# Batch 0's recurrent state summed by TensorE and decayed by ScalarE, pair 2's narrowing moved, late low-rank additions

## The chip, the cores and the metric

One core of one Trainium2 chip. The metric is the device time of one execution in microseconds; the kernel before has a median of 706.71 us over 3 runs (705.61 to 708.09).

## The reference, cut to what matters

The program is a gated linear attention over 4 batches, 8 heads, 768 positions and head dimension 48, followed by two mixing layers:

```python
f = 1 / (1 + exp(-f_logit))
for t in range(S):
    state = f[t][:, None] * state + outer(k[t], v[t])     # per batch and head, 48x48
    y[t] = q[t] @ state
x = heads side by side                                     # (B, 768, 384)
u = x + (x.transpose(0, 2, 1) @ U @ V).transpose(0, 2, 1)  # rank 32 over the positions
x = u + maximum(u @ w_ch1, 0) @ w_ch2                      # 384 -> 1536 -> 384
h = gelu(x @ w_in); u, v = halves of h                     # 384 -> 1024
x = x + (u * (w_sg @ layernorm(v) * g + b_sg)) @ w_out
```

Inputs are float32; the weights come as 64-bit words that hold doubles and are narrowed to float32 on the chip.

## The kernel before, in words

**Attention.** Each batch is cut into 6 chunks of 128 positions (NCH). Within a chunk the recurrence is turned into matrix products: two scans on VectorE, `a_decay` (L333, products of the forget gates backwards, g) and `a_grow` (L350, their inverse), scale k and q; `a_scores` multiplies k and q on TensorE (L365), masks the scores (`am`, VectorE L371, for batch 0 one half by ScalarE L373 and GpSimd L374) and transposes k (L379, L381). `a_out` forms y = am x v (L392) + q x T (L397), copies it to `x` (ScalarE, L400) and forms k'v (L412). T is the state, a tile of 112 partitions by 4 pairs of heads by 96 columns: head j of a pair stands in rows 64j to 64j+47 and columns 48j to 48j+47, all else in T is zero from the start (L186). `a_state` adds k'v to T (VectorE L426, one operation per j) and multiplies by the decay of the next chunk, `fall` (L428, one per j); in chunk 0 it only multiplies. `a_xt` transposes x into xT, and `low_rank_sum` adds x^T U into one PSUM bank (L458), whose sum after the last chunk becomes `hs`, high part on ScalarE (L468) and low part on VectorE (L469). `low_rank_out` then adds hs V to one half of the positions of xT in three products of 384 columns (L478) with an addition on VectorE each (L480). f32 products are run as two passes of the array, f32r products as one.

**Order.** The order of all instructions is written out by hand (`tc.manual_schedule`), each engine runs its own in order. For batch 0 the loop of L537 to L562 issues, for chunk c: the scans of chunk c+2, the scores of c+1, the transposition of c-1, the low-rank sum of c-2, the outputs and k'v of c, the state of c, and in between the narrowing of early weights: `use_first` (ScalarE L250 spreads the high words, VectorE L246 shifts the low ones), `use_middle` (VectorE L255, L256 merge them, two halves of 128x384 per pair), `use_last` (high part on ScalarE L285, low part on GpSimd L287). "Pair i" is the i-th of 12 pairs of w_ch1 and w_ch2 blocks of 128 hidden units. Pairs 1 and 2 are narrowed ahead of chunk 5's output. `warm(n)` issues n products with the identity that nobody reads (L520).

**MLP.** After the attention of batch 0 come the first low-rank additions, `make_hl` (the input's high parts on ScalarE L145 and low parts on VectorE L146), and the MLP of batch 0: per half of the positions 12 groups f; group f has 9 products into bank "h" (L80), a relu to `ah` (ScalarE L511), the low part `al` (VectorE L512), and the 9 products of the group before into three "ch" banks (L495). After each group `fill` issues more work. For batch 0 that is `narrow_ahead(f)`: the merge of pair f+3 out of PSUM, the high and low parts of pair f+2, the spread of pair f+4 into two "at" banks (L250) and its shift; from group 9 on also the attention of batch 1, which uses the old form of `a_state`. PSUM has 2 banks "h", 3 "ch" and 3 "at", each set used in turn.

Of the kernel before, what the change touches and what calls it, by code (L numbers as in the profile page):

```python
# [12 lines left out]
ACTF = mybir.ActivationFunctionType  # L13
# [4 lines left out]
B, H, S, D = 4, 8, 768, 48  # L18
# [3 lines left out]
NP = H // 2  # L22
# [4 lines left out]
KD = DM // 128  # L27
# [3 lines left out]
PR = 112  # L31
# [20 lines left out]
def kernel(  # L52
# [16 lines left out]
    vec, act, pool, pe = nc.vector, nc.scalar, nc.gpsimd, nc.tensor  # L69

    keep = ctx.enter_context(tc.tile_pool(name="keep", bufs=1))
    ident = keep.tile([128, 128], F32, name="ident")
# [59 lines left out]
    def fast(st):  # L132
# [7 lines left out]
        def bank(kind, shape):  # L140
            n = {"h": 2, "ch": 3, "at": 3}[kind]
            return ps.tile(shape, F32, tag=kind, bufs=n, name="ps_" + kind)

        def split(hi, lo, src, eng=pool):
            act.activation(hi, src, ACTF.Copy)  # L145
            eng.tensor_tensor(lo, src, hi.bitcast(F32), op=ALU.subtract)  # L146
# [6 lines left out]
        def make_hl(work, b, hf, eng=pool):  # L153
            hi = work.tile([128, KD, HT], F32R, tag="uh", name="uh")
            lo = work.tile([128, KD, HT], F32R, tag="ul", name="ul")
            for kd in range(KD):
                split(hi[:, kd], lo[:, kd], xT[b][:, kd, hf * HT:(hf + 1) * HT], eng)
            hl[b, hf] = (hi, lo)
# [23 lines left out]
        T = cst.tile([PR, NP, 2 * D], F32, name="T")  # L182
# [9 lines left out]
        def kind(b):  # L192
            return "at" if b else "ch"

        def room(b, c):
            if b == 0 and c > 2:
                x = flat(xT[6 - c])
                t, vv = x[0:PR, 0:QW], x[:, QW:QW + DM]
            else:
                t = ld.tile([PR, QW], F32, tag="fqk", name="fqk")  # L200
                vv = ld.tile([128, DM], F32, tag="v", name="v")
            tiles[b, c] = dict(t=t, v=vv)
            return t, vv

        def load(b, c):
            t, vv = room(b, c)
            for x in range(0, QW, QW // 2):
                nc.sync.dma_start(t[:, x:x + QW // 2], fqk[b, c, :, x:x + QW // 2])
            nc.sync.dma_start(vv, v[b, c * C:(c + 1) * C, :])
# [34 lines left out]
        def shift(i):  # L244
            for low, _ in raws[i]:
                vec.tensor_scalar(low, low, 29, None, op0=ALU.logical_shift_right)  # L246

        def spread(i, zs):
            for z, (_, high) in zip(zs, raws[i]):
                act.activation(z, high.bitcast(F32), ACTF.Copy, scale=2.0 ** -112)  # L250

        def merge(i, dst, zs):
            for d, z, (low, high) in zip(dst, zs, raws[i]):
                di, zi = d.bitcast(I32), z.bitcast(I32)
                vec.scalar_tensor_tensor(zi, zi, 3, low, op0=ALU.logical_shift_left, op1=ALU.bitwise_or)  # L255
                vec.scalar_tensor_tensor(di, high, -2 ** 31, zi, op0=ALU.bitwise_and, op1=ALU.bitwise_or)  # L256
# [3 lines left out]
        def z_tiles(i):  # L260
            z = zs.tile([128, 2, UNIT], F32, tag="z", name="z")
            n = NCH * R if i == "u" else UNIT
            return [z[:, x, :n] for x in range(len(raws[i]))]

        def use_first(i):
            ready[i] = z_tiles(i)
            spread(i, ready[i])
            shift(i)

        def use_middle(i):  # L270
            merge(i, ready[i], ready[i])
# [83 lines left out]
        def a_scan(b, c):  # L355
            a_decay(b, c)
            a_grow(b, c)
# [27 lines left out]
        def a_out(b, c):  # L385
            e = tiles[b, c]
            vv = e["v"]
            y = bank(kind(b), [128, DM])
            half = [slice(i, i + C // 2) for i in range(0, C, C // 2)]
            for h in range(H):  # L390
                for t in half:
                    pe.matmul(y[t, h * D:(h + 1) * D], lhsT=e["am"][h % 2][:, h // 2, t],  # L392
                              rhs=vv[:, h * D:(h + 1) * D], start=(h == 0), stop=(c == 0 and h == H - 1))
            if c:
                for p in range(NP):
                    for t in half:
                        pe.matmul(y[t, p * 2 * D:(p + 1) * 2 * D], lhsT=e["q"][:, p, t], rhs=T[:, p, :],  # L397
                                  start=False, stop=(p == NP - 1))
            x = aw.tile([128, DM], F32, tag="x", name="x", bufs=3)
            act.activation(x, y, ACTF.Copy)  # L400
            if b:
                xh[b, c] = aw.tile([128, DM], F32R, tag="xh", name="xh", bufs=3)
                xl[b, c] = aw.tile([128, DM], F32R, tag="xl", name="xl", bufs=3)
                split(xh[b, c], xl[b, c], x)
            else:
                xh[b, c] = x
            if c < NCH - 1:
                kv = bank(kind(b), [PR, NP, D])
                for p in range(NP):
                    for j in range(2):  # L410
                        rows = slice(64 * j, 64 * j + D)
                        pe.matmul(kv[rows, p, :], lhsT=e["kt"][:, p, rows],  # L412
                                  rhs=vv[:, (2 * p + j) * D:(2 * p + j + 1) * D], start=True, stop=True)
                e["kv"] = kv
            e["x"] = x

        def a_state(b, c):
            e = tiles[b, c]
            fall = tiles[b, c + 1]["fall"]
            parts = []  # L420
            for j in range(2):
                rows = slice(64 * j, 64 * j + D)
                parts.append((T[rows, :, j * D:(j + 1) * D], e["kv"][rows], fall[rows].to_broadcast([D, NP, D])))
            if c:
                for Tj, kv, _ in parts:
                    vec.tensor_tensor(Tj, kv, Tj, op=ALU.add)  # L426
            for Tj, kv, fj in parts:
                vec.tensor_tensor(Tj, Tj if c else kv, fj, op=ALU.mult)  # L428

        def a_xt(b, c):  # L430
            x = tiles[b, c]["x"]
            xp = bank(kind(b), [128, KD, C])
            for d in range(KD):
                pe.transpose(xp[:, d, :], x[:, d * 128:(d + 1) * 128], ident)
            act.activation(xT[b][:, :, c * C:(c + 1) * C], xp, ACTF.Copy)
            del tiles[b, c]
# [35 lines left out]
        def low_rank_out(b, hf, where="at"):  # L472
            for d in range(KD):
                low_rank_add(b, hf, d, where)

        def low_rank_add(b, hf, d, where):
            t = bank(where, [128, HT])
            pe.matmul(t, lhsT=hs[b][:, d * 128:(d + 1) * 128], rhs=vs[:, hf * HT:(hf + 1) * HT], start=True, stop=True)  # L478
            dst = xT[b][:, d, hf * HT:(hf + 1) * HT]
            vec.tensor_tensor(dst, t, dst, op=ALU.add)  # L480
# [36 lines left out]
        def warm(n, w=3):  # L517
            t = bank("h", [128, w, 128])
            for _ in range(n):
                pe.matmul(t, lhsT=ident, rhs=ident[:, None, :].to_broadcast([128, w, 128]), start=True, stop=True)  # L520
# [16 lines left out]
        for c in range(NCH):  # L537
            if c + 2 < NCH:
                a_scan(0, c + 2)
            if c - 1 in early:  # L540
                use_last(early[c - 1])
            if c + 1 < NCH:
                a_scores(0, c + 1)
            if c:
                a_xt(0, c - 1)
            if c > 1:
                low_rank_sum(0, c - 2)
            if c > 1 and c in early:
                use_first(early[c])
                use_middle(early[c])  # L550
            elif c == NCH - 1:
                low_rank_sum(0, c - 1)
                for i in (1, 2):
                    use_first(i)
                    use_middle(i)
            a_out(0, c)
            warm(1, 2)
            if c + 1 < NCH:
                a_state(0, c)
            if c == 0:  # L560
                use_first("u")
                use_middle("u")  # L562
        low_rank_sum(0, NCH - 1)
        use_last(1)
        a_xt(0, NCH - 1)
        warm(2)
        low_rank_out(0, 0)
        make_hl(work, 0, 0, vec)
        load(1, 0)
        load(1, 1)  # L570
        get(*range(3, KF1))
# [10 lines left out]
                load(nb, nc3)  # L582

        def narrow_ahead(f):
            if f == 0:
                low_rank_out(0, 1, "ch")
            if f + 3 < KF1:
                bank_middle(f + 3)
            if f + 2 < KF1:
                use_last(f + 2)  # L590
            if f + 4 < KF1:
                bank_first(f + 4)
# [371 lines left out]
```

## Time and profile before

| | |
|---|---|
| median of 3 runs | 706.71 us (705.61 to 708.09) |
| the profiled execution | 708.97 us, span 707.2 us, mean granted TensorE clock 0.986 |
| TensorE busy | 684.7 us (97%) |
| VectorE busy | 444.2 us (63%) |
| ScalarE, GpSimd busy | 260.1 us (37%), 242.3 us (34%) |
| attention of batch 0 | 0 to about 57 us |
| MLP of batch 0 begins | about 58.7 us |

The busy shares are means over the whole span; the stages differ. In the rows below PE is TensorE, PEld its weight loads, DVE VectorE, ACT ScalarE, POOL GpSimd. A row of the timeline merges instructions of one kind that follow each other (x2, x16), and the text in brackets is how long the engine idled before it and what released it. The clock is a share of the full 2.4 GHz.

### The profile page before, as it was taken

The numbers are of one execution on the slowest core, as the hardware profiler recorded it, in microseconds if no ns is written. First come the engines' busy times: TensorE is split into PE (matmuls) and PEld (weight loads), VectorE is DVE, ScalarE is ACT, GpSimd is POOL, SyncE is SP. The second block draws the span as 40 slices with busy tenths as digits, with TensorE's granted clock in tenths as the row PEclk, the third lists the DMA queues.
The fourth block names the chain that finished last, engine by engine and source line by source line (L and its number), as shares of the span: only waits on it lengthen the run. The fifth ranks groups of instructions, "written<-read, shape, count | busy, mean of one in ns | idle before, by whom it ended". The sixth has DMA issues, their size and how long they took to land.

```text
span 707.2 us, 12716 instructions
## 1 busy us (share of the span) xinstructions
PE 684.7 (97%) x5151; PEld 647.9 (92%) x5151; DVE 444.2 (63%) x808; ACT 260.1 (37%) x526; POOL 242.3 (34%) x262
## 2 busy tenths in 40 slices
PE   8977988999999999999999999999999999999997
PEld 5757988999999999999999999999999989999996
DVE  7998997654476545566547961387585377458532
ACT  3444732323232222323324433455335154233410
POOL 4543652112231111221203543566353344326030
PEclk9998999999999999999999999999999999999999
DMA  9994011232112130111004422100010001001001
GB/s 229 315 358 147 0 38 46 72 103 51 52 51 52 51 99 4 52 52 51 2 1 121 120 85 68 34 1 1 0 62 7 1 0 68 1 1 46 22 1 71
DMA packets 21010, 44.90 MB, mean 63 GB/s; under 512 B 2544, under 2 KB 10352, under 8 KB 20944
## 3 DMA queue, kind: packets, MB, share of 16 engines
q1 hardware_dynamic: 20944, 44.01, 20.9%
q8 instruction: 42, 0.69, 0.4%
q14 instruction: 24, 0.20, 0.1%
HBM read 39.28 MB, written 4.72 MB: 62 GB/s over the span
## 4 chain that ended last, share of the span: by engine, by line
PE 85%; DVE 11%; issue 1%; DMA 1%; POOL 1%; ACT 1%; SPq 0%; DVEq 0%; ACTq 0%; POOLq 0%
PE ps_h L80 28%; PE ps_ch L495 18%; PE ps_ch L80 13%; PE ps_at L80 13%; PE ps_at L365 3%; PE ps_at L392 3%; DVE z L256 2%; PE ps_at L397 1%; DVE ps_at L255 1%; PE ps_at L379 1%; DVE raw L246 1%; DVE g L333 1%; PE ps_at L458 1%; DVE al L512 1%; DMA fqk<-in_fqk_dram 1%
## 5 line engine op out<-in xcount | busy, mean ns | idle before, releaser
L512 DVE SCALAR_TENSOR_TENSOR al<-ps_h,ah 128x384 fp32r<-128x384 f32 x96 | 53.3, 556 | 112.5 <-ACT ah L511 112.1
L80 PE MATMUL ps_h<-uh,w 128*128 128x384 f32 x576 | 122.7, 348 | 1.2 <-POOL w L287 0.7
L495 PE MATMUL ps_ch<-ah,w 128*128 128x384 f32 x576 | 115.4, 334 | 0.9 <-ACT ah L511 0.9
L80 PEld LDWEIGHTS ps_h<-uh,w 128*128 128x128 f32 x576 | 100.6, 191 | 3.9 <-ACT uh L145 1.4
L495 PEld LDWEIGHTS ps_ch<-ah,w 128*128 128x128 f32 x576 | 101.3, 188 | 1.2 <-ACT ah L511 1.2
L511 ACT ACTIVATE ah<-ps_h 128x384 fp32r<-128x384 f32 x96 | 47.1, 490 | 124.7 <-PE ps_h L80 123.6
L341 POOL TENSOR_TENSOR fqk<-fqk,g 112x512 f32<-112x512 f32 x21 | 27.2, 1294 | 150.7 <-DVE g L333 119.0
L80 PE MATMUL ps_h<-ul,w 128*128 128x384 f32 x288 | 66.2, 338 | 0.0
L495 PE MATMUL ps_ch<-al,w 128*128 128x384 f32 x288 | 65.7, 335 | 0.1
L146 POOL TENSOR_TENSOR ul<-xT,uh 128x384 fp32r<-128x384 f32 x45 | 46.9, 1068 | 47.4 <-ACT uh L145 46.5
L146 POOL TENSOR_TENSOR gtl<-t,gth 128x384 fp32r<-128x384 f32 x32 | 32.8, 1027 | 73.4 <-ACT gth L145 73.4
L80 PEld LDWEIGHTS ps_h<-ul,w 128*128 128x128 f32 x288 | 52.4, 191 | 0.0
L495 PEld LDWEIGHTS ps_ch<-al,w 128*128 128x128 f32 x288 | 51.2, 188 | 0.4 <-DVE al L512 0.4
L145 ACT ACTIVATE gth<-t 128x384 fp32r<-128x384 f32 x32 | 16.8, 525 | 78.0 <-DVE t L741 78.0
L371 DVE TENSOR_TENSOR am<-ps_at,mask 128x512 f32<-128x512 f32 x42 | 27.2, 684 | 19.4 <-PE ps_at L365 19.2
L146 POOL TENSOR_TENSOR vnl<-t,vnh 128x512 fp32r<-128x512 f32 x24 | 31.1, 1296 | 17.8 <-ACT vnh L145 17.8
L146 POOL TENSOR_TENSOR xl<-x,xh 128x384 fp32r<-128x384 f32 x18 | 18.2, 1011 | 54.3 <-ACT xh L145 52.4
L80 PE MATMUL ps_ch<-w,vnh 128*128 128x384 f32 x144 | 36.6, 335 | 0.1
L80 PE MATMUL ps_at<-w,vnh 128*128 128x384 f32 x144 | 36.6, 334 | 0.0
L287 POOL TENSOR_TENSOR w<-z,w 128x384 fp32r<-128x384 f32 x24 | 25.0, 1064 | 23.8 <-ACT w L285 20.3
L365 PEld LDWEIGHTS ps_at<-fqk 48*128 48x128 f32 x336 | 21.4, 187 | 10.4 <-issue 9.2
L365 PE MATMUL ps_at<-fqk 48*128 48x128 f32 x336 | 25.5, 285 | 4.6 <-DVE T L428 1.4
(221 smaller groups left out, 1496.2 us busy)
## 6 DMA issues: line engine op xcount, KB each, us to landing
fqk<-in_fqk_dram SPq DMA_DIRECT2D x38, 339.5 KB, 4.1
raw<-in_w_dram SPq DMA_DIRECT2D x24, 384.0 KB, 7.9
out_dram<-xT SPq DMA_DIRECT2D x24, 192.0 KB, 2.0
v<-in_v_dram SPq DMA_DIRECT2D x21, 192.0 KB, 4.5
raw<-in_w_in_dram SPq DMA_DIRECT2D x8, 384.0 KB, 3.3
z<-in_w_sg_dram SPq DMA_DIRECT2D x12, 192.0 KB, 2.4
xT<-in_fqk_dram SPq DMA_DIRECT2D x6, 339.5 KB, 9.0
raw<-in_w_out_dram SPq DMA_DIRECT2D x4, 384.0 KB, 3.2
```

The source lines that it names most:

```text
L80: pe.matmul(ps, lhsT=l, rhs=r, start=(i == 0), stop=(i == n - 1))
L145: act.activation(hi, src, ACTF.Copy)
L146: eng.tensor_tensor(lo, src, hi.bitcast(F32), op=ALU.subtract)
L256: vec.scalar_tensor_tensor(di, high, -2 ** 31, zi, op0=ALU.bitwise_and, op1=ALU.bitwise_or)
L287: pool.tensor_tensor(t[:, 1], s, t[:, 0].bitcast(F32), op=ALU.subtract)
L341: pool.tensor_tensor(k, k, g.rearrange("p h t -> p (h t)"), op=ALU.mult)
L365: pe.matmul(sc[j][:, p, :], lhsT=e["k"][rows, p, :], rhs=e["q"][rows, p, :], start=True, stop=True)
L371: vec.tensor_tensor(am, sc[j], m3, op=ALU.mult)
L392: pe.matmul(y[t, h * D:(h + 1) * D], lhsT=e["am"][h % 2][:, h // 2, t], rhs=vv[:, h * D:(h + 1) * D], start=(h == 0), stop=(c == 0 and h = ...
L495: pe.matmul(ch[d], lhsT=w, rhs=a[i // 2], start=(f == 0 and i == 0), stop=(last and i == 2))
L511: act.activation(ah, hp, ACTF.Relu)
L512: vec.scalar_tensor_tensor(al, hp, 0.0, ah.bitcast(F32), op0=ALU.max, op1=ALU.subtract)
```

## The change

For batch 0 alone, `a_out` makes the k'v bank as wide as T and opens it with two products of the identity and T, rows 0 to 63 and 64 to 111, so that k'v is accumulated onto T in PSUM. `a_state` then is four ScalarE copies, one per pair of heads, out of the bank into T, scaled by `fall`. The warm-up product after each chunk's output is dropped, and one of two after the last transposition. Pair 2's spread, shift and merge are issued behind `make_hl` and no longer ahead of chunk 5's output. The additions to the second half of xT, all three in group 0 with "ch" banks before, are issued one each in groups 2, 3 and 4 with "at" banks.

```diff
--- before.py
+++ after.py
@@ -405,18 +405,26 @@
             else:
                 xh[b, c] = x
             if c < NCH - 1:
-                kv = bank(kind(b), [PR, NP, D])
+                kv = bank(kind(b), [PR, NP, D] if b else [PR, NP, 2 * D])
+                if not b:
+                    for rows in (slice(0, 64), slice(64, PR)):
+                        pe.matmul(kv[rows], lhsT=ident[:PR, rows], rhs=T, start=True, stop=False)
                 for p in range(NP):
                     for j in range(2):
                         rows = slice(64 * j, 64 * j + D)
-                        pe.matmul(kv[rows, p, :], lhsT=e["kt"][:, p, rows],
-                                  rhs=vv[:, (2 * p + j) * D:(2 * p + j + 1) * D], start=True, stop=True)
+                        pe.matmul(kv[rows, p, :] if b else kv[rows, p, j * D:(j + 1) * D], lhsT=e["kt"][:, p, rows],
+                                  rhs=vv[:, (2 * p + j) * D:(2 * p + j + 1) * D], start=bool(b),
+                                  stop=bool(b) or p == NP - 1)
                 e["kv"] = kv
             e["x"] = x
 
         def a_state(b, c):
             e = tiles[b, c]
             fall = tiles[b, c + 1]["fall"]
+            if not b:
+                for p in range(NP):
+                    act.activation(T[:, p, :], e["kv"][:, p, :], ACTF.Copy, scale=fall[:, p, :])
+                return
             parts = []
             for j in range(2):
                 rows = slice(64 * j, 64 * j + D)
@@ -550,11 +558,9 @@
                 use_middle(early[c])
             elif c == NCH - 1:
                 low_rank_sum(0, c - 1)
-                for i in (1, 2):
-                    use_first(i)
-                    use_middle(i)
+                use_first(1)
+                use_middle(1)
             a_out(0, c)
-            warm(1, 2)
             if c + 1 < NCH:
                 a_state(0, c)
             if c == 0:
@@ -563,9 +569,11 @@
         low_rank_sum(0, NCH - 1)
         use_last(1)
         a_xt(0, NCH - 1)
-        warm(2)
+        warm(1)
         low_rank_out(0, 0)
         make_hl(work, 0, 0, vec)
+        use_first(2)
+        use_middle(2)
         load(1, 0)
         load(1, 1)
         get(*range(3, KF1))
@@ -582,8 +590,8 @@
                 load(nb, nc3)
 
         def narrow_ahead(f):
-            if f == 0:
-                low_rank_out(0, 1, "ch")
+            if 2 <= f < 2 + KD:
+                low_rank_add(0, 1, f - 2, "at")
             if f + 3 < KF1:
                 bank_middle(f + 3)
             if f + 2 < KF1:
```

## Rows read from the trace of the kernel before

**Rows 1.** The page's chain by engine; the chain in order of time (start, us, what).
```profile
PE 85%; DVE 11%; issue 1%; DMA 1%; POOL 1%; ACT 1%; SPq 0%; DVEq 0%; ACTq 0%; POOLq 0%
...
33.80 1.23 DVE g L333
112.70 1.13 PE ps_at L365 x14
```

**Rows 2.** Busy time of each engine in two stretches: length, engines, clock, DMA.
```profile
36.00:54.00 18.00, 13.57 (x155) 9.33 (x153) 17.34 (x32) 8.31 (x18) 8.36 (x8) 0.91 1.03 363
200.00:707.00 507.00, 501.83 (x3453) 484.47 (x3451) 293.20 (x527) 180.32 (x360) 167.49 (x186) 1.00 0.13 39
```

**Rows 3.** The same in two stretches of 3 us.
```profile
39.00:42.00 3.00, 3.00 (x19) 2.08 (x15) 2.87 (x6) 1.20 (x3) 0.87 (x2) 0.50 1.01 330
57.00:60.00 3.00, 2.44 (x6) 1.57 (x7) 2.42 (x6) 1.83 (x5) 0.00 (x0) 0.50 1.04 233
```

**Rows 4.** The tile T up to 60 us: line, engine, operation, minimum/median/maximum ns.
```profile
L426 DVE TENSOR_TENSOR T<-ps_ch,T x8: 340/352/362, 23.2 to 47.4; 48x192 f32<-48x192 f32 x8
L428 DVE TENSOR_TENSOR T<-T,fall x8: 350/356/1284, 24.0 to 48.2; 48x192 f32<-48x192 f32 x8
```

**Rows 5.** Timeline, chunks of batch 0, VectorE and GpSimd: start us, us, engine, line.
```profile
23.81 1.27 POOL L374 TENSOR_TENSOR am<-am,mask 128x512 f32<-128x512 f32 x1
24.01 1.67 DVE L428 TENSOR_TENSOR T<-T,fall 48x192 f32<-48x192 f32 x2
33.80 1.22 DVE L333 TENSOR_TENSOR_SCAN g<-ps_at,gone 112x511 f32<-112x511 f32 x1
```

**Rows 6.** Timeline, nearest rows for the added operations on TensorE and ScalarE.
```profile
20.63 0.85 PE L397 MATMUL ps_ch<-T,fqk 112*64 112x96 f32 x16
...
51.88 1.46 PE L520 MATMUL ps_h<-ident 128*128 128x384 f32 x4
...
21.90 0.70 PE L520 MATMUL ps_h<-ident 128*128 128x256 f32 x2
...
16.76 0.38 ACT L250 ACTIVATE z<-raw 128x192 f32<-128x192 f32 x1
...
52.14 0.93 ACT L285 ACTIVATE w<-z 128x384 fp32r<-128x384 f32 x2
```

**Rows 7.** Timeline, a sigmoid and the products of chunk 4.
```profile
30.36 0.59 ACT L326 ACTIVATE ps_at<-xT 112x512 f32<-112x512 f32 x1
...
38.47 1.86 PE L365 MATMUL ps_at<-xT 48*128 48x128 f32 x16 [2.23 <-POOL xT L352]
42.08 1.02 ACT L250 ACTIVATE z<-raw 128x384 f32<-128x384 f32 x2
43.95 0.53 PE L412 MATMUL ps_ch<-xT,kt 128*48 128x48 f32 x16
```

**Rows 8.** Timeline, VectorE from pair 2 to the low parts of the MLP's input.
```profile
54.28 1.34 DVE L255 SCALAR_TENSOR_TENSOR z<-z,raw 128x384 int32<-128x384 int32 x1
56.25 0.55 DVE L469 TENSOR_TENSOR hs<-ps_h,hs 32x384 fp32r<-32x384 f32 x1
58.98 1.48 DVE L146 TENSOR_TENSOR ul<-xT,uh 128x384 fp32r<-128x384 f32 x3
```

**Rows 9.** Timeline, MLP groups 0 to 5 of batch 0.
```profile
62.84 0.56 DVE L512 SCALAR_TENSOR_TENSOR al<-ps_h,ah 128x384 fp32r<-128x384 f32 x1 [1.84 <-ACT ah L511]
63.31 1.48 DVE L480 TENSOR_TENSOR xT<-ps_ch,xT 128x384 f32<-128x384 f32 x3
67.44 0.55 DVE L512 SCALAR_TENSOR_TENSOR al<-ps_h,ah 128x384 fp32r<-128x384 f32 x1
69.16 0.53 ACT L250 ACTIVATE ps_at<-raw 128x384 f32<-128x384 f32 x1 [1.03 <-DVE z L256]
69.64 0.56 DVE L256 SCALAR_TENSOR_TENSOR z<-raw,ps_at 128x384 int32<-128x384 int32 x1
80.25 0.55 DVE L512 SCALAR_TENSOR_TENSOR al<-ps_h,ah 128x384 fp32r<-128x384 f32 x1
```

## The prediction

> **What bounds the kernel now.** I read the summary of the chain of waits first: TensorE holds 85% of it, VectorE 11% [rows 1]. The windows say where the VectorE part lies. From 200 us to the end TensorE is busy 501.8 of 507 us, so an edit ahead of that stretch can only move it as a whole. In 36 to 54 us VectorE is busy 17.34 of 18 us, TensorE 13.57, ScalarE 8.31, GpSimd 8.36 [rows 2]. The chain in order of time then runs over VectorE, with short exceptions, from the scan at 33.80 to 112.6 us, and over TensorE from 112.70 us [rows 1, 5]. So until 112 us VectorE's own list is the clock of the kernel, and after it VectorE has slack and TensorE carries any shift to the end. I therefore follow VectorE through five checkpoints: the scan of chunk 5 (33.80), the low part of hs (56.25), and the subtraction `al` of MLP groups 0, 1 and 5 (62.84, 67.44, 80.25) [rows 5, 8, 9]. Every start below is from the profiled execution (708.97 us, span 707.2); it is 2.3 us over the median 706.71, and I take the difference over to the median unchanged.
>
> **Part 1, the state.** VectorE loses 18 half-updates (chunk 0: two; chunks 1 to 4: four each). Eight adds at 0.352 and ten products at 0.356 us are 6.4 us [rows 4], more where a product stood behind GpSimd: the pair at 24.01 took 1.67 us beside GpSimd's product of 23.81 [rows 5]. Such a stall may only pass to the next VectorE operation on SBUF.
>
> TensorE gains two f32 products per chunk, T through the identity, of 384 columns, 64 and 48 rows of output wide. Four passes of 384 columns took 1.46 us, 0.32 a pass apart from the tail, so 1.28 us if nothing overlaps [rows 6]. The q x T products, also in halves of 64, ran 16 passes of 96 columns in 0.85 us: about 0.04 a pass, where 96 of 384 columns would make 0.08, so neighbouring halves do overlap [rows 6], which gives 0.64. With only two in a row one pass at each end stays alone: I take 0.96 and keep 0.64 to 1.28. The warm-up product that goes had 0.70 us [rows 6] but stood behind k'v; its absence gives nothing where the next scores wait for GpSimd anyway.
>
> ScalarE gains four copies of 112x96 per chunk, scaled per partition. No row shows that form. The nearest are the copy of 128x192 at 0.38 and two of 128x384 in 0.93 where one alone is 0.52 us [rows 6]: 0.73 ns an element, 0.11 overlap. One of 96 is then 0.31, four 4x0.31-3x0.11 = 0.91 us. Above stands 4x0.38 = 1.5; below, nothing, where ScalarE idles beside it. I take 0.91, as the rows are close in shape. These rows have constant scales. The Trainium skill (ScalarE: Activation LUTs, What ACT_TABLE_LOAD costs) adds about 93 ns for each per-partition pointer operand; no run here shows one. By it the four take 0.37 us more, twice on the path worked out next, and the gain below would be 2.8 instead of 3.5 us.
>
> What queues behind these copies decides more than their length. ScalarE works in order, and in the program the sigmoid of chunk c+3 follows the state of chunk c; VectorE's scan waits for it. Before, chunk 5's sigmoid began at 30.36, right behind the 0.49 us copy of y [rows 7]. Now T-add 0.96, k'v 0.53 and the copies 0.91 follow y, with the copy of y beside the first: 30.36-0.49+0.96+0.53+0.91 = 32.3, plus 0.59 for the sigmoid: the scan starts at 32.85, not 33.80. Of the roughly 4 us that VectorE was spared up to there (chunks 0 to 2, a stall with them) it gets 0.95; the rest is now waiting for ScalarE. The next binding state is chunk 4's. TensorE went from the scores of chunk 5 at 38.47 to the end of k'v at 44.48 [rows 7]; 0.95 earlier and with T-add this ends at 44.5, the copies at 45.4. Behind them ScalarE has two high parts of pair 0 (0.93), x transposed (0.48), two spreads of pair 1 (1.0, as at 42.08) and the copy of y (0.49): 48.3. The last low-rank sum (0.8) and the copy to hs (0.5) follow, and VectorE's low part of hs starts at about 50.0. VectorE itself is through with pair 1 by 49.6, so both are late together.
>
> **Part 2, pair 2.** Its two shifts and four merges (2x0.31+4x0.56 = 2.9 us free; 4.2 there, one merge 1.34 beside GpSimd) stood ahead of hs at 56.25 [rows 8]. Without them and with part 1 that is 50.0, 6.2 us earlier. From hs to the end of the three low parts `ul` it was 58.98+1.48-56.25 = 4.2 us [rows 8], so 54.2. Then come pair 2 (2.9) and the shifts of pair 3 (0.6): the first `al` at 57.7. Before, VectorE idled 1.84 us ahead of that `al`, since the first products ran at the lower clock [rows 9, 3]; now pair 2 covers them. TensorE's first group, ready by about 55, waits for nothing else, and no DMA is moved: the weights' transfers are issued in the same order. The warm-up product dropped here falls into the same cover. So `al` of group 0 is 5.1 us earlier. If GpSimd's low parts of pairs 1 and 2 block VectorE here, it costs up to 1 us.
>
> **Part 3, the late additions.** The three additions to the second half (1.48 us) stood behind `al` of group 0 and go to groups 2, 3 and 4: between groups 0 and 1 VectorE saves them (4.6 us there before, 3.2 in each of the next four, (80.25-67.44)/4) [rows 9]. So group 1's `al` comes at 60.9, group 2's at 64.1, 6.5 us early. In the sum over six groups the move itself gives nothing, 0.5 is paid in each of three groups. But the addition now takes one of the three "at" banks, in which the next pair's two spreads also lie. Before, the ring left one bank free, and the second spread waited only for the first merge of the pair before (0.53 us at 69.16, idle 1.03 for it). Now both wait, the second for the last merge, 69.64+0.55 in the rows' place; the spread and the next relu follow on ScalarE, 0.45 and 0.5 us, and `al`, which started 1.0 after that merge's start, starts 1.5 after it [rows 9]. That is 0.5 us in each of three groups. VectorE's period is 4.2 there; TensorE's 3.3 fits into it. The end of group 4 pays 3x(0.5+0.5) = 3.0: `al` of group 5 at 64.1+9.6+3.0 = 76.7 against 80.25. **Sum: 3.5 us earlier**, 705.5 for the profiled execution, 703.2 for the median. Groups 5 to 11 and the first chunks of batch 1 keep their order, and so the shift.
>
> **The rivals.**
> - *No ring wait.* If the spreads need less time or VectorE finds its next shift first, 1.5 us of part 3 go, and the gain is 5 to 6: about 701.2. For: ScalarE has over 1 us of idle in each group. Against: that idle lies just where the spread waits now.
> - *The state's way over TensorE and ScalarE is dearer.* T-add unshared and partly at the lower clock (1.9) and copies of 0.38 each (1.5) make 0.96+0.6 = 1.55 us more in chunks 2 and 4: 3.1 of the 3.5 are lost, about 706.3, no change. For: the clock stood at 0.50 in 39 to 42 us [rows 3]. Against: T-add sits in a dense run of products.
> - *The change does not spare VectorE anything*, because every freed slot turns into a stall behind GpSimd: the same place, the same time.
> - *Slower: the lower clock holds through the attention stage.* TensorE loses ten warm-up passes and now sits on the loop scores, y, T-add, k'v, T, sigmoid, scan. If it runs at 1.2 GHz from 24 us to hs, chunk 2's state is 3.2 us later than forecast (scan at 36.1), the scores of chunk 5 start at 40.4 and take, with sums, y, T-add and k'v, 9.6 us: T at 51, and hs near 58.7 instead of 50.0. The gain of 3.5 becomes a loss of 5.2: 712. It decides once more than about two fifths of that stretch are slow. For: 0.50 followed idle stretches in 39 to 42 and 57 to 60 us [rows 3]. Against: T-add is longer than the warm-up it replaces, and TensorE's waits for GpSimd get shorter. The Trainium skill (TensorE: Matmul & The Clock Gate, What's actually happening) calls the slow state the default that activity lifts, which would make dropped warm-ups a price; the rows at 0.50 agree.
>
> **How the numbers follow.** Forecast 0.53 (701.8 to 704.8 from the bounds of the copies and of the stall at pair 2), no ring wait 0.20, dearer way and unspared VectorE together 0.17, slower 0.10. About 0.3%, 2.1 us, can be told from no change. Faster by more than that (under 704.6): nearly all of the first two, 0.70; same 0.20; slower 0.10. The range 700.2 to 707.0 leaves out the slow case and the tails of the others.
>
> **What would show it.** No L426 or L428 before 100 us; VectorE idle ahead of chunk 4's and 5's scans, ended by a sigmoid; hs near 50 us; no idle ahead of the first `al`; groups 2 to 4 with a period near 4.2 us and `al` waiting for the relu; one shift from group 5 to the end. Wrong it would be if the scans start without a wait (then more is won), if the granted clock is at 0.50 over several windows of the chunks, or if the shift at group 5 is not the shift at the end.

## The result, and the profile after

The changed kernel takes 700.04 us (median of 4 runs, 699.13 to 701.85) against 707.18 us: ratio 0.9904, 95% interval 0.9876 to 0.9933, and 0.9898 (0.9877 to 0.9919) when it was timed again (e9). It is 7.1 us faster where 3.5 were forecast, and 700.04 lies 0.2 us below the range that the prediction gave. The sign and the place were right, and the mechanism but for one step (a wait for banks in part 3); the forecast size was half of the measured one. The profiled execution took 701.85 us, span 700.0. One execution of the kernel before (1347.62 us, in the set of e5 to e8) and one of e8 (950.41 us) were far longer than all others, and the ratios leave them out.

The head of the profile after, whose last line answers to the first of [rows 1]:

```profile
PE 680.6 (97%) x5157; PEld 643.1 (92%) x5157; DVE 436.3 (62%) x790; ACT 265.0 (38%) x546; POOL 241.8 (35%) x262
...
PE 84%; DVE 10%; DMA 4%; issue 1%; ACT 1%; SPq 0%; DVEq 0%; ACTq 0%
```

The windows after, answering to [rows 2, 3], with 24 to 30 us and 105 to 111 us added (length, then busy time of PE, PEld, DVE, ACT, POOL, then clock, DMA share, GB/s):

```profile
24.00:30.00 6.00, 6.00 (x107) 4.79 (x103) 5.65 (x8) 3.30 (x11) 4.66 (x4) 1.00 1.04 356
...
36.00:54.00 18.00, 15.36 (x172) 11.41 (x170) 16.57 (x30) 12.57 (x30) 6.94 (x7) 1.00 1.04 345
...
105.00:111.00 6.00, 5.40 (x32) 5.21 (x33) 3.69 (x7) 1.10 (x3) 0.23 (x1) 0.72 0.02 4
...
200.00:700.00 500.00, 494.68 (x3360) 477.69 (x3358) 288.50 (x520) 177.71 (x355) 165.18 (x184) 1.00 0.13 40
```

The same stretch before, which the prediction did not show and on which its size hung:

```profile
24.00:30.00 6.00, 6.00 (x85) 4.80 (x87) 5.86 (x9) 2.10 (x5) 3.66 (x4) 0.72 1.03 387
```

VectorE's share of 36 to 54 us fell from 17.34 to 16.57 us, ScalarE's rose from 8.31 to 12.57, and TensorE's clock is 1.00 in 24 to 30 and 36 to 54 us, where it was 0.72 and, in 39 to 42, 0.50 [rows 3]. The end did not change: from group 5's `al` to the end of the span it is 626.95 us before and 626.85 after. All of the gain lies ahead of that `al`.

The slow stretch is a matter of the execution and not of the old form. Chunk 3's scan and the copy of chunk 2's y behind it, before:

```profile
19.58 1.22 DVE L333 TENSOR_TENSOR_SCAN g<-ps_at,gone 112x511 f32<-112x511 f32 x1
...
29.97 0.49 ACT L400 ACTIVATE x<-ps_ch 128x384 f32<-128x384 f32 x1 [2.41 <-PE ps_ch L397]
```

The same rows in the trace of e2, an experiment below that has the old state too, and its clock in 24 to 30 us:

```profile
19.26 1.22 DVE L333 TENSOR_TENSOR_SCAN g<-ps_at,gone 112x511 f32<-112x511 f32 x1
...
28.06 0.48 ACT L400 ACTIVATE x<-ps_ch 128x384 f32<-128x384 f32 x1
...
24.00:30.00 6.00, 5.30 (x93) 4.18 (x91) 5.76 (x10) 2.87 (x6) 3.67 (x4) 1.00 1.03 365
```

The copy stands 10.39 us behind the scan before and 8.80 in e2 (8.80 in e3 as well); after it is 8.89.

The timeline after, chunks (columns: start us, us, engine, line; in brackets the idle time before and what ended it), answering to [rows 5 to 7]. L411 is T-add, L426 the state copies, L415 k'v, L477 the low part of hs, L520 `al`:

```profile
15.94 0.82 PE L411 MATMUL ps_ch<-T,ident 112*64 112x384 f32 x4
...
16.59 0.53 PE L415 MATMUL ps_ch<-v,kt 128*48 128x48 f32 x16
...
17.23 1.03 ACT L426 ACTIVATE T<-ps_ch,fall 112x96 f32<-112x96 f32 x4 [0.59 <-PE ps_ch L415]
...
19.24 1.22 DVE L333 TENSOR_TENSOR_SCAN g<-ps_at,gone 112x511 f32<-112x511 f32 x1
...
24.13 1.22 DVE L333 TENSOR_TENSOR_SCAN g<-ps_at,gone 112x511 f32<-112x511 f32 x1 [1.14 <-ACT ps_at L326]
...
28.13 0.47 ACT L400 ACTIVATE x<-ps_ch 128x384 f32<-128x384 f32 x1
...
29.09 1.03 ACT L426 ACTIVATE T<-ps_ch,fall 112x96 f32<-112x96 f32 x4 [0.48 <-PE ps_ch L415]
...
30.00 0.62 ACT L326 ACTIVATE ps_at<-xT 112x512 f32<-112x512 f32 x1
...
30.72 1.22 DVE L333 TENSOR_TENSOR_SCAN g<-ps_at,gone 112x511 f32<-112x511 f32 x1
...
35.38 1.16 PE L365 MATMUL ps_at<-xT 48*128 48x128 f32 x16 [1.05 <-POOL xT L352]
...
39.89 0.53 PE L415 MATMUL ps_ch<-xT,kt 128*48 128x48 f32 x16
```

T-add costs 0.65 us from its start to that of k'v, the lower bound of the prediction: its halves overlap. Four copies take 1.03 us. The scan of chunk 4 waits 1.14 us for its sigmoid, which stands behind the copies, as forecast. Chunk 5's scan starts at 30.72 instead of 33.80, and without the wait that the prediction named: its sigmoid ends at 30.62, and VectorE comes from its list at about the same time.

From hs into the MLP, answering to [rows 8, 9]:

```profile
42.62 2.25 DVE L246 TENSOR_SCALAR raw<-raw 128x384 int32<-128x384 int32 x2
...
45.98 0.49 ACT L476 ACTIVATE hs<-ps_h 128x384 fp32r<-128x384 f32 x1 [1.00 <-PE ps_h L466]
...
47.03 0.55 DVE L477 TENSOR_TENSOR hs<-ps_h,hs 32x384 fp32r<-32x384 f32 x1
...
49.52 1.49 DVE L146 TENSOR_TENSOR ul<-xT,uh 128x384 fp32r<-128x384 f32 x3
...
53.30 2.31 POOL L287 TENSOR_TENSOR w<-z,w 128x384 fp32r<-128x384 f32 x2 [4.39 <-ACT w L285]
...
53.59 2.24 DVE L246 TENSOR_SCALAR raw<-raw 128x384 int32<-128x384 int32 x2
...
55.75 0.54 DVE L520 SCALAR_TENSOR_TENSOR al<-ps_h,ah 128x384 fp32r<-128x384 f32 x1
...
62.15 0.55 DVE L520 SCALAR_TENSOR_TENSOR al<-ps_h,ah 128x384 fp32r<-128x384 f32 x1
...
63.19 0.52 ACT L250 ACTIVATE ps_at<-raw 128x384 f32<-128x384 f32 x1 [0.79 <-DVE xT L488]
...
63.74 0.55 DVE L256 SCALAR_TENSOR_TENSOR z<-raw,ps_at 128x384 int32<-128x384 int32 x1
...
64.33 0.52 ACT L250 ACTIVATE ps_at<-raw 128x384 f32<-128x384 f32 x1 [0.61 <-DVE z L256]
...
65.81 0.55 DVE L520 SCALAR_TENSOR_TENSOR al<-ps_h,ah 128x384 fp32r<-128x384 f32 x1
...
73.15 0.55 DVE L520 SCALAR_TENSOR_TENSOR al<-ps_h,ah 128x384 fp32r<-128x384 f32 x1
```

hs comes at 47.03 instead of 56.25. Its high part is ready on ScalarE at 46.47; VectorE's list is the later branch by 0.56 us, and in it the two shifts of pair 1 take 2.25 us (0.62 free) beside GpSimd's low parts of pair 0, which began at 42.34. The first `al` follows after 8.72 us; 1.6 of them are the shifts of pair 3, which take 2.24 us (0.62 free) because GpSimd began its low parts of pair 2 0.3 us earlier. Groups 2 to 4 have a period of 3.67 us, and their `al` does not wait.

The checkpoints as distances from one to the next. Chunk 2's scan starts at 13.40 us before and at 12.70 after, and between 12.21 and 14.09 in the twelve traces of the experiments, though the code up to there is all but the same; in most of them it waits for a transfer. In the new form chunk 3's scan does not move with it: it stands behind the state copies of chunk 0 on ScalarE, and comes at 19.24 in the trace after, in e6 and in e9, where chunk 2's comes at 12.70, 12.21 and 13.19. So chunk 3's scan is the better point to count from. The prediction has no time of its own for it; its column takes the one of before (19.58).

| from, to | before | forecast | after |
|---|---|---|---|
| chunk 2's scan to chunk 5's | 20.40 | 19.45 | 18.02 |
| of this, chunk 3's scan to chunk 5's | 14.22 | 13.27 | 11.48 |
| chunk 5's scan to hs | 22.45 | 17.15 | 16.31 |
| hs to `al` of group 0 | 6.59 | 7.7 | 8.72 |
| group 0 to group 2 | 7.80 | 6.4 | 6.40 |
| group 2 to group 5 | 9.61 | 12.6 | 11.00 |
| group 5 to the end of the span | 626.95 | 626.95 | 626.85 |

### The profile page after: what moved, and what is told of

Read it like the earlier page. It is cut to its first block, busy times and chain, and to the rows that moved or that the text cites. A ratio compares the mean times of both kernels' runs of the same rounds, so it can differ in the third digit from the quotient of the medians.

```text
span 700.0 us, 12736 instructions
## 1 busy us (share of the span) xinstructions
PE 680.6 (97%) x5157; PEld 643.1 (92%) x5157; DVE 436.3 (62%) x790; ACT 265.0 (38%) x546; POOL 241.8 (35%) x262
## 4 chain that ended last, share of the span: by engine, by line
PE 84%; DVE 10%; DMA 4%; issue 1%; ACT 1%; SPq 0%; DVEq 0%; ACTq 0%
PE ps_h L80 28%; PE ps_ch L503 19%; PE ps_ch L80 13%; PE ps_at L80 13%; PE ps_at L365 3%; PE ps_at L392 3%; DVE z L256 2%; DVE raw L246 2%; PE ps_at L397 1%; DMA xT<-in_fqk_dram 1%; DMA raw<-in_w_v_dram 1%; DVE ps_at L255 1%; PE ps_at L379 1%; PE ps_at L466 1%; DVE z L255 1%; DVE al L520 1%
## 5 line engine op out<-in xcount | busy, mean ns | idle before, releaser
L520 DVE SCALAR_TENSOR_TENSOR al<-ps_h,ah 128x384 fp32r<-128x384 f32 x96 | 53.3, 555 | 110.6 <-ACT ah L519 110.2
L126 DVE TENSOR_SCALAR t<-t,mv,rs 128x512 f32<-128x512 f32 x24 | 20.8, 866 | 12.3 <-POOL rs L125 12.3
```

Source lines behind the costliest of these rows:

```text
L126: vec.tensor_scalar(dst, src, mv[:, 0:1], rs, op0=ALU.subtract, op1=ALU.mult)
L520: vec.scalar_tensor_tensor(al, hp, 0.0, ah.bitcast(F32), op0=ALU.max, op1=ALU.subtract)
```

## The experiments

Each is timed in five rounds beside the kernel before, on the same chip as its neighbours in its set (e1 to e4, e5 to e8, e9 to e12). The ratio is to the kernel before, in brackets its 95% interval.

**e1 and e2: the two halves alone.** e1 is the kernel before with the new `a_out` and `a_state` alone (the diff's first hunk), e2 with pair 2 moved alone:

```diff
-                for i in (1, 2):
-                    use_first(i)
-                    use_middle(i)
+                use_first(1)
+                use_middle(1)
...
         make_hl(work, 0, 0, vec)
+        use_first(2)
+        use_middle(2)
```

> The new state (added in PSUM, decayed by ScalarE) alone; pair 2, the warm-up products and the additions to the second half as before. Theory S, the 18 half-updates taken from VectorE carry most of the gain: pair 2 (2.9 us) still stands ahead of hs, so hs near 50 instead of 56.3, group 5's al near 74.5 instead of 80.25, 5 to 6 us faster in all. Rival P, moving pair 2 carries it and the state only waits for ScalarE instead: hs at 53 or later, 2 us or less.

> Pair 2's narrowing moved behind the first low parts, nothing else. Theory S: y of chunk 5 still waits for T on VectorE until 49.3, so hs cannot come before about 52.3 (56.25 before); the 4 us won there are paid back by pair 2 behind it except for the 1.8 us in which VectorE idled ahead of the first al and a stall: 1 to 2.5 us faster. Rival P: 4 us or more.

e1: 704.01 us, ratio 0.9949 (0.9933 to 0.9965), 3.7 us faster. e2: 708.44 us, 1.0007 (0.9992 to 1.0022), no change. So the state carries half of the gain and moving pair 2 carries nothing alone; with the state, it is worth the other half (0.9949 to 0.990), as e4 and e11 leave nothing measurable to the other parts. For e2 I had expected 1 to 2.5 us, which did not come. The two traces show why. e1, from hs's high part on:

```profile
46.79 0.49 ACT L476 ACTIVATE hs<-ps_h 128x384 fp32r<-128x384 f32 x1 [1.00 <-PE ps_h L466]
...
49.10 1.34 DVE L255 SCALAR_TENSOR_TENSOR z<-z,raw 128x384 int32<-128x384 int32 x1
...
51.07 0.55 DVE L477 TENSOR_TENSOR hs<-ps_h,hs 32x384 fp32r<-32x384 f32 x1
...
53.32 2.58 PE L80 MATMUL ps_h<-uh,w 128*128 128x384 f32 x6 [0.72 <-ACT uh L145]
...
57.42 0.56 DVE L520 SCALAR_TENSOR_TENSOR al<-ps_h,ah 128x384 fp32r<-128x384 f32 x1 [1.84 <-ACT ah L519]
```

hs is ready on ScalarE at 47.28, but VectorE, still at pair 2, takes its low part at 51.07; TensorE waits, its first products then run at the lower clock (0.58 in 54 to 60 us), and VectorE idles 1.84 us ahead of the first `al`, as before [rows 9]. e2:

```profile
52.64 0.49 ACT L468 ACTIVATE hs<-ps_h 128x384 fp32r<-128x384 f32 x1 [1.94 <-PE ps_h L458]
...
53.16 0.55 DVE L469 TENSOR_TENSOR hs<-ps_h,hs 32x384 fp32r<-32x384 f32 x1 [1.42 <-ACT hs L468]
...
59.82 2.29 POOL L287 TENSOR_TENSOR w<-z,w 128x384 fp32r<-128x384 f32 x2 [4.25 <-ACT w L285]
...
60.11 2.23 DVE L246 TENSOR_SCALAR raw<-raw 128x384 int32<-128x384 int32 x2
...
62.25 0.55 DVE L512 SCALAR_TENSOR_TENSOR al<-ps_h,ah 128x384 fp32r<-128x384 f32 x1
```

Here y of chunk 5 still waits for T on VectorE, so hs has its high part only at 53.13 and VectorE idles 1.42 us for it. The low part is 3.1 us earlier than before; the moved pair and the shifts of 2.23 us beside GpSimd take all but 0.6 of that by the first `al`. Moving work off a path pays when what is left on the path is ready earlier; each edit removes one of two branches that end at the same hs. My expectation for e1 (5 to 6 us) was too high by 1.3 to 2.3 us against the timed runs; in its trace group 5's `al` stands at 74.84, as expected (74.5).

**e3 and e11: the late additions, alone and taken back.** e3 puts only the last hunk of the diff into the kernel before; e11 takes it out of the changed one (this is e11's edit):

```diff
-            if 2 <= f < 2 + KD:
-                low_rank_add(0, 1, f - 2, "at")
+            if f == 0:
+                low_rank_out(0, 1, "ch")
```

> The additions to the second half of xT in groups 2, 3 and 4, nothing else. As forecast, with a wait of the second spread for the last merge: groups 2 to 4 take 4.2 us, 3.0 us paid for 1.4 saved, 1.5 us slower. Rival, as the trace after reads (groups of 3.67 us, the spread waits for the addition and the first merge only): 1.4 saved and 3 x 0.47 paid, no change within 0.5 us.

> The changed kernel with the three additions back in group 0 and its ch banks. If late additions carry part of the gain (in the changed kernel pair 2 fills VectorE ahead of group 0): 1.4 us come back between groups 0 and 1, 3 x 0.47 us go from groups 2 to 4, so group 5's al within 0.3 us of the changed kernel: no change. Rival, the additions in group 0 stop TensorE, whose next products wait for the ch banks behind pair 2: 1 to 2 us slower.

e3: 708.63 us, 1.0012 (0.9992 to 1.0032). e11: 701.91 us, 0.9898 (0.9874 to 0.9922), like the changed kernel beside it (0.9898). The late additions are worth nothing measurable in either form: 1.4 us leave group 0 and 3 x 0.47 come back in groups 2 to 4. The 0.5 us of waiting that I put on each of these groups isn't there. In the trace after, the first spread starts 0.03 us after the addition ends (63.16) and the second 0.04 us after the first merge (64.29), not after the last one; e3's trace has the same order. This fits banks that are handed out as they come free, where the addition's own bank is the first to. It does not fit banks used in turn.

**e4: the warm-up products back**, in the changed kernel (`warm(1, 2)` after `a_out`, `warm(2)` before the low-rank additions).

> The changed kernel with all warm-up products back (one after each chunk's output, two before the first low-rank additions). If they only fill TensorE's waits: within 0.7 us of the changed kernel, about 6.5 to 7 us faster than before, the clock at 1.00 up to 60 us as without them. Rival, they lie on the loop of scores, y and k'v now: 5 x 0.43 us, about 2 us slower than the changed kernel. Rival, without them the clock is at risk: 1 us faster than the changed kernel.

702.13 us, 0.9925 (0.9907 to 0.9943); the intervals of the changed kernel overlap with it. From chunk 3's scan to hs it takes 27.79 us, as in the trace after: they lie in TensorE's waits and cost nothing there. Whether they cost 1 us elsewhere the runs don't tell.

**e5: pair 3's shift first**, in the changed kernel:

```diff
         make_hl(work, 0, 0, vec)
-        use_first(2)
-        use_middle(2)
         load(1, 0)
         load(1, 1)
         get(*range(3, KF1))
         bank_first(3)
+        use_first(2)
+        use_middle(2)
```

> The changed kernel with the spread and shift of pair 3 issued ahead of pair 2's narrowing. In the trace after, pair 3's two shifts take 2.24 us (0.62 free) beside GpSimd's low parts of pair 2, and the first al comes only behind them. If that stall is a price of its own, the first al starts 1 to 1.6 us earlier behind the low part of hs (8.7 us there now) and the kernel is 1 us faster than the changed one. Rival, the block passes to pair 2's last merge, which then stands beside the same GpSimd work: no change.

699.92 us, 0.9879 (0.9859 to 0.9898): by the ratio 1.3 to 1.8 us under the changed kernel (0.9898, 0.9904), about as expected, though the intervals overlap.

```profile
50.74 1.17 DVE L246 TENSOR_SCALAR raw<-raw 128x384 int32<-128x384 int32 x4
...
53.46 0.56 DVE L256 SCALAR_TENSOR_TENSOR z<-raw,z 128x384 int32<-128x384 int32 x1
...
53.65 2.22 POOL L287 TENSOR_TENSOR w<-z,w 128x384 fp32r<-128x384 f32 x2 [4.93 <-ACT w L285]
...
53.94 0.55 DVE L520 SCALAR_TENSOR_TENSOR al<-ps_h,ah 128x384 fp32r<-128x384 f32 x1
```

The four shifts run free (1.17 us), and GpSimd starts when the last merge is already under way: 7.10 us from hs to the first `al` instead of 8.72. The stall was a price of its own in the trace after. It isn't the same in every execution: in the second trace of the changed kernel (e9) the shifts began 0.14 us ahead of GpSimd and took 1.45 us, in e11's 0.26 us ahead and took 0.62. Two engines arrive within 0.3 us of each other, and who is first decides over up to 1.6 us.

**e6: the sigmoid of chunk c+3 ahead of the state copies of chunk c**, in the changed kernel (`a_gate` is the first part of `a_decay`: the bank and the sigmoid).

```diff
             a_out(0, c)
+            if c + 3 < NCH:
+                a_gate(0, c + 3)
             if c + 1 < NCH:
                 a_state(0, c)
```

> The changed kernel with the sigmoid of chunk c+3 issued on ScalarE ahead of the four state copies of chunk c. Theory queue: the scan of chunk 4, which idled 1.14 us for its sigmoid, starts 1 us earlier, and so does all behind it: 1 us faster than the changed kernel. Rival load: the next narrowing waits for its transfer (the first half of V lands at 27.6 us, where VectorE and ScalarE both wait), so the 1 us is lost there: chunk 5's scan at 30.5 to 30.9 as now, no change.

701.96 us, 0.9901 (0.9882 to 0.9921): not told from the changed kernel. The trace has a gain all the same. Chunk 4's scan starts without a wait (22.90), 3.66 us behind chunk 3's instead of 4.89. At chunk 5's scan 0.81 of these 1.23 us are left (29.91, 10.67 behind chunk 3's instead of 11.48), and 0.82 at hs and at group 5's `al`, counted in the same way against the trace after. That is 0.1% of the time, too little for these runs to tell. The load theory had the transfer of V take all of it. In this trace V's narrowing began at 26.74 without a wait; instead the small operation behind chunk 4's scan now stands beside GpSimd's product (0.62 us instead of 0.17), which takes 0.45. So the timed outcome is the rival's, and its reason is not what the trace shows.

**e7: the decay on VectorE**, T still added by TensorE:

```diff
-                for p in range(NP):
-                    act.activation(T[:, p, :], e["kv"][:, p, :], ACTF.Copy, scale=fall[:, p, :])
+                for j in range(2):
+                    rows, cols = slice(64 * j, 64 * j + D), slice(j * D, (j + 1) * D)
+                    vec.tensor_tensor(T[rows, :, cols], e["kv"][rows, :, cols], fall[rows].to_broadcast([D, NP, D]),
+                                      op=ALU.mult)
```

> The changed kernel with T still added by TensorE, but the decay as two VectorE products per chunk (ten in all, 0.36 us each, 3.6 us) in place of the ScalarE copies. If VectorE's list is the clock: 1.5 to 3 us slower than the changed kernel, since some of the 3.6 us falls into VectorE's waits for sigmoids (1.1 and 0.6 us). Rival, the loop over TensorE and ScalarE is the clock now: the copies' 1.03 us per chunk go from it, and it is as fast or faster.

702.0 us, 0.9910 (0.9890 to 0.9930): not told from the changed kernel. The 1.5 to 3 us that a VectorE list without room would have cost are not there; the rival came true. Chunk 5's scan comes 11.72 us after chunk 3's (11.48), hs 16.30 later (16.31). The ten products fit into waits that VectorE has in the changed kernel, so the copies on ScalarE bring no measurable part of the gain. What is left for the state's 3.7 us are the eight adds, the step that they put between k'v and T, and stalls: before, two of the pairs of products took 1.67 and 1.47 us beside GpSimd, and in e7, where they read k'v's bank instead of T, every pair takes 0.71 to 0.72. The runs do not tell these three apart.

**e8: no warm-up product at all**, the changed kernel without `warm(7)`, `warm(4)` and `warm(1)`.

> The changed kernel without any warm-up product, the 11 before the first chunks and the last one too. Theory clock: the forecast was too small because it took the times of TensorE's products from a stretch at 0.72 of the clock (24 to 30 us), where the changed kernel has 1.00; with the clock at 0.5 to 0.75 somewhere in 10 to 36 us, the scan of chunk 5 comes 1 to 2 us later relative to the scan of chunk 2 (18.0 us now), and the gain over before falls to 3.5 to 5.5 us. Rival: the new products keep the clock up alone, no change within 0.7 us.

702.71 us, 0.9922 (0.9903 to 0.9940): by the ratio 5.5 us faster than before, the upper end of what the clock theory gave, with an interval that overlaps with the changed kernel's.

```profile
12.48 2.08 PE L365 MATMUL ps_at<-fqk 48*128 48x128 f32 x16 [1.12 <-DVE am L371]
...
19.43 1.04 ACT L426 ACTIVATE T<-ps_ch,fall 112x96 f32<-112x96 f32 x4 [1.52 <-PE ps_ch L415]
...
20.77 0.36 DVE L255 SCALAR_TENSOR_TENSOR z<-z,raw 128x192 int32<-128x192 int32 x1 [3.24 <-ACT z L250]
...
21.44 1.21 DVE L333 TENSOR_TENSOR_SCAN g<-ps_at,gone 112x511 f32<-112x511 f32 x1
```

The scores of chunk 1 take 2.08 us instead of 1.16, the state of chunk 0 comes at 19.43 instead of 17.23, VectorE idles 3.24 us for what stands behind it on ScalarE, and chunk 3's scan comes at 21.44 instead of 19.24. So in the new form a slow TensorE shows in VectorE's list at once, 2.2 us for one chunk. From 21 us on the products run at their usual length, and chunk 3's scan to hs takes 27.78 us, as in the trace after. By the first `al` (56.30, 7.08 behind hs) part of the loss is hidden, as pair 3's shifts came ahead of GpSimd in this trace and took 0.64 us.

**e9 and e10: the changed kernel again, and with its chunks 2 and 4 made longer.** e9 is the control for its set. e10 adds three products that nobody reads:

```diff
                 if not b:
+                    if c in (2, 4):
+                        warm(3)
                     for rows in (slice(0, 64), slice(64, PR)):
```

> The changed kernel itself, on the same chip as the three runs beside it: 0.990 of the time before, 6 to 8 us faster.

> The changed kernel with three idle products of 384 columns (0.64 us each, 1.9 us in all) on TensorE between q x T and T-add of chunks 2 and 4, the two chunks that the lower clock had made longer in the profile of before. If TensorE's time on the way to the state is the term that the forecast mis-sized: chunk 2's state, the sigmoid behind it and chunk 5's scan come 1.9 us later (18.0 us behind chunk 2's scan now, then 19.5 to 20, the forecast's distance), the low part of hs 2 to 3 us later, and about half of the 7 us is lost: 3 to 5 us faster than before. Rival, the state has slack and the gain is VectorE's alone: scan and hs within 0.5 us, no change against the changed kernel.

e9: 701.08 us, 0.9898. e10: 705.63 us, 0.9957 (0.9940 to 0.9975), 2.9 us faster than before, at the edge of the 3 to 5 expected.

```profile
27.75 2.20 PE L530 MATMUL ps_h<-ident 128*128 128x384 f32 x6
...
31.22 1.03 ACT L428 ACTIVATE T<-ps_ch,fall 112x96 f32<-112x96 f32 x4 [2.86 <-PE ps_ch L417]
...
32.12 0.62 ACT L326 ACTIVATE ps_at<-xT 112x512 f32<-112x512 f32 x1
...
32.84 1.22 DVE L333 TENSOR_TENSOR_SCAN g<-ps_at,gone 112x511 f32<-112x511 f32 x1 [2.24 <-ACT ps_at L326]
...
50.53 0.55 DVE L479 TENSOR_TENSOR hs<-ps_h,hs 32x384 fp32r<-32x384 f32 x1
...
76.66 0.55 DVE L522 SCALAR_TENSOR_TENSOR al<-ps_h,ah 128x384 fp32r<-128x384 f32 x1
```

Counted from chunk 3's scan (19.09 here), chunk 2's state comes 12.13 us later where e9 has 9.85, 2.3 us more, and the sigmoid and the scan behind it follow one for one (13.75 against 11.47). hs is at 50.53 and group 5's `al` at 76.66. The forecast had 13.27 for that distance, and 50.0 and 76.7: with TensorE slowed in these two chunks by 2.2 us each, somewhat more than the profile before showed (1.6), the forecast's chain comes out near its numbers, and the timed gain of 2.9 us is near its 3.5. In the last figure two errors nearly cancel (GpSimd's stall at pair 3's shifts, the bank wait that isn't there). e10 shows that TensorE's time lies on the path here; that the lower clock had made it longer in the profile before is shown by the rows of e2, not by e10.

**e12: the three lessons together**: e5, e6, and the first half of V fetched ahead of chunk 5's input.

```diff
+        get("v0")
         load(0, 5)
-        get("v0", "v1", 0, 1, 2)
+        get("v1", 0, 1, 2)
```

> The changed kernel with pair 3's spread and shift ahead of pair 2's narrowing, the sigmoid of chunk c+3 ahead of the state copies of chunk c, and the first half of V fetched ahead of chunk 5's input, so that its landing no longer ends the wait at 27.6 us. If the three add up: the first al 1.8 us earlier by the shift, 0.7 to 1.1 by the sigmoid: 2 to 3 us faster than the changed kernel. Rival, V ahead of chunk 5 delays chunk 5's input or the sum is bound by TensorE's loop: as fast as the shift alone, 1 us or less.

698.63 us (698.54 to 700.12), 0.9864 (0.9841 to 0.9887): the fastest of all, 9.9 us under before and 2.5 us under the changed kernel beside it, within the 2 to 3 expected, though the intervals of the two still touch. Its trace has chunk 5's scan 10.67 us behind chunk 3's, as e6, hs 16.30 later, and the first `al` 7.10 behind hs, as e5: the two add up. V's earlier transfer shows no part of it, as from chunk 4's scan to chunk 5's it is 7.01 us in e6 and here.

## Why the prediction was right, and where its size was off

- **What bounds** held for the kernel before: the stretch ahead of 112 us was the place, and the shift at group 5 (7.10 us) is the shift at the end (7.2 us). In the new form VectorE's list is no longer alone the clock of the chunks: chunk 4's scan waits for ScalarE, and e7's ten products find room. Two of the signs did not come. Chunk 5's scan and the `al` of groups 2 to 4 start without a wait, the case for which the prediction said that more is won.
- **Part 1, the state: the mis-sized term.** The chain T-add, k'v, copies, sigmoid was right, and its own length was near. From the start of y's copy to the end of chunk 2's copies I had 0.96+0.53+0.91 = 2.40 us; it took 30.12-28.13 = 1.99 (T-add is 0.3 shorter and starts 0.3 ahead of y's copy, k'v and copies are 0.1 longer each). What was off above all is the time from which it counts. The prediction took it from [rows 7], where the sigmoid at 30.36 stands right behind y's copy, and that copy stands behind a stretch with the clock at 0.72, 10.39 us behind chunk 3's scan. It is 8.89 after, 8.78 in e9, and 8.80 in e2 and e3, which have the old state and the clock at 1.00 in 24 to 30 us. So about 1.5 us of it came with that execution and not with the old form. The 6.0 us for chunk 4's products, 38.47 to 44.48, held the 0.50 of [rows 3] as well; after they took 5.04 with T-add in them (35.38 to 40.42). In the old form this cost nothing, as VectorE was later than TensorE anyway: from chunk 3's scan to chunk 5's it is 14.22 us before, and 14.21 and 14.23 in e2 and e3. So the slow stretch was TensorE's slack, and a duration out of a slack is no price for a path. e10 puts some 2 us back into each of the two chunks and gets near the forecast's checkpoints, e8 shows 2.2 us for one slow chunk. The trace's group 5 is 3.6 us ahead of the forecast: 0.3 by chunk 3's scan, 1.8 up to chunk 5's (1.4 of it y's copy, 0.4 the chain), 0.8 from there to hs and 1.6 by part 3, less 1.0 at pair 2. The state of chunk 4 came 1.9 us earlier behind chunk 5's scores than forecast; only 0.8 reach hs, where VectorE's list, with the stall at pair 1, is the later branch.
- **The weighed rule** of the Trainium skill (ScalarE: Activation LUTs, What ACT_TABLE_LOAD costs), a surcharge for each per-partition operand: one copy took 0.341 us (median of 20). ScalarE's copies out of PSUM with a constant scale took 0.49 for 384 columns and 0.58 to 0.60 for 512, which makes an estimated 0.24 to 0.29 for 96: a surcharge of 0.05 to 0.10, and the rule's 0.09 agrees. I had extrapolated from copies out of SBUF (0.31), so the four, at 1.03, are 0.12 over my 0.91 and under the 1.28 that rule and rows together gave.
- **Part 2, pair 2.** hs came first and pair 2 covered the first products, as forecast. From hs to the first `al` it was 1.0 us over the forecast's 7.7: a stall of 1.6 us at pair 3's shifts, of the kind that I had named (up to 1) and left out of the sum. e5 takes it away. That the move alone is worth nothing (e2) the prediction had not said; it follows from its own working, in which both hs branches ended at 50.0 us.
- **Part 3, the late additions.** The step "the second spread waits for the last merge" was wrong, 1.6 us: 3.67 us per group, not 4.2. It followed from the banks being used in turn, which the section on the kernel says too, and which the order of the spreads in the traces after and of e3 contradicts.
- **The rivals.** "No ring wait" named 701.2 us and came nearest; it is what happened in part 3, but alone it would have given half of the difference. The slow rival's mechanism is real (e8), its condition didn't arise. The dearer way was wrong in both prices (T-add 0.65, four copies 1.03). Of the unspared rival two places are seen, the shifts of pairs 1 and 3, each 1.6 us longer beside GpSimd; most of what was spared stayed spared.

## What to carry to other kernels

Before a duration is put on a path, look whether it was on the path in the trace from which it is taken: a slow clock or a wait inside another engine's slack is not a price, and it may not come again. When two branches end at the same instruction, moving one alone may give nothing (pair 2) and be worth several us together with the other; test them together before dropping either. Where two engines that block each other arrive within a few tenths of a microsecond, issue the blocked work first: both traces in which that was done (e5, e12) have 7.10 us from hs to the first `al`, where the changed kernel has 7.93 and 8.72.

## What the runs showed of the hardware that was not expected

The granted clock in the record is 1.00 from 6 to 18 us of e8, where the scores of chunks 0 and 1 took 2.08 us and the same products later 1.16, 1.8 times less; there the durations speak for the lower level, which the clock's column doesn't show. The lower level came at the same code in some executions and not in others: 24 to 30 us stood at 0.72 before and at 1.00 in e2 and e3, 105 to 111 us at 0.72 after and 1.00 in e9. From group 5's `al` to the end the six traces with 0.72 or 0.74 in a stretch near 105 to 117 us took 626.9 to 628.4 us (mean 627.7), the eight without 625.4 to 626.6 (626.2): 1.5 us that no edit here explains, and as much as some of the differences above. What sets it off was not tried.
